# Attention, a dense layer and eight experts on one core: the softmax sums' reciprocals side by side, and the tails' transpose in another PSUM bank

## The chip, the cores and the metric

The kernel runs on one core of one Trainium2 chip. The metric is the device time of one execution in microseconds, as a median of several runs. A profile is one execution taken by the hardware profiler; its span goes from the first to the last instruction.

## The reference

All tensors are float32. The first of three parts is the one that the change touches.

```python
def _attn_ref(q, k, v):                       # 4 batches, 8 heads, 576 positions, 64 features
    scores = scale * np.matmul(q, k.transpose(0, 1, 3, 2))
    mask = block_i >= block_j                 # blocks of 64 positions, block-causal
    scores = np.where(mask, scores, -1000000000.0)
    scores = scores - np.max(scores, axis=-1, keepdims=True)
    attn = np.exp(scores)
    attn = attn / (np.sum(attn, axis=-1, keepdims=True) + 1e-09)
    return np.matmul(attn, v)
...
x = attn_out.transpose(0, 2, 1, 3).reshape(2304, 512)
h = x @ w_in                                  # 512 x 2048
x = np.maximum(0.01 * h, h) @ w_out           # 2048 x 512
P = exp(x @ w_gate - max), 8 rounds of row and column normalisation
out = sum over 8 experts of P[:, e] * (relu(x @ w1[e]) @ w2[e])
```

## The kernel before

Attention works on pairs of heads: 4 batches x 4 pairs = 16 pairs, two heads of 64 features on the 128 partitions. A pair's 576 positions are nine blocks of 64. The loop over pairs p (L471) is software-pipelined over four pairs at once: `prv` = p - 1, `cur` = p, `nxt` = p + 1 and `fol` = p + 2. The list `turns` (L437) is the order in which PE takes one turn of that loop, written out by hand; the order of the other engines and of the DMA queue is made by the framework's planner, from modelled costs.

In one turn, in PE's order: the scores of `nxt` for block 8 and its exponentials; group 0 of the transposed exponentials of `cur`; products of `prv` with v; scores 3 and 2; the rest of the products of `prv`, then `split_x`; group 1; scores 5 and 4; group 2; `turn_q` of `fol`; scores 1 and 0; `turn_tail` of `fol`; the first product of `cur` (L402 and the first of L405); group 3; scores 7 and 6; `turn_k` of `fol`; groups 4, 5 and 6.

`turn_q`, `turn_k` and `turn_tail` transpose q, k and the last 64 positions of both on PE. ACT copies the q side from PSUM into qT (L278), DVE the k side into kT (L283). `turn_attn` transposes 25 pieces of the exponentials in seven groups of four (the last holds one) and copies each group into `at`, even groups on ACT (L390), odd ones on DVE (L392).

A row's sum of exponentials comes out of ACT's exponential, one column of `ssum` for each block. `totals` (at the head of a turn) adds 1e-9 on POOL, takes the reciprocal on DVE (L358) and writes the result to a DRAM tile, the blocks of even and of odd number in a transfer each (L362). `spread_totals` reads each half back with a broadcast over 64 partitions (`by_feature`, four transfers, L371). `split_x` (L414) multiplies the product by it on DVE on its way out of PSUM, and then splits the result into two parts (L424, L425) that the dense layer uses.

PSUM has eight banks: three for scores (`ps_sc`), three for transposes (`ps_tr`, tag `tr`), and one tile of two banks for the product (`ps_av`, tile `av`), in its first bank columns 0 to 127 for the tails, 128 to 255 for the last group of turned rows and 384 to 511 for the first product.

All transfers of this part are issued by SyncE (SP) on one queue, one after the other: q, tails and k three pairs ahead, v, rows, by_feature, and raw weights for the dense layer, whose preparation runs in small steps between the scores. An instruction of SP that waits holds up all that stand behind it.

Behind attention follow the dense layer (L513, L533) and the experts, which the change does not touch.

Of the kernel before, what the change touches and what calls it, by code (L numbers as in the profile page):

```python
# [8 lines left out]
F32 = mybir.dt.float32  # L9
# [6 lines left out]
P = 128  # L16
# [20 lines left out]
def block_attention_mlp_moe(  # L37
# [15 lines left out]
    nc = tc.nc  # L53
# [4 lines left out]
    NQ = S // BLK  # L58
# [156 lines left out]
    def attention(att, ps_sc, ps_tr, ps_av):  # L215
# [13 lines left out]
        ex = [att.tile([P, ew], F32, name=f"ex{i}") for i in range(2)]  # L229
        nmax = [att.tile([P, NQ + 1], F32, name=f"nmax{i}") for i in range(2)]  # L230
        ssum = [att.tile([P, NQ + 1], F32, name=f"ssum{i}") for i in range(2)]
        rsum = [att.tile([P, NQ], F32, name=f"rsum{i}") for i in range(2)]
        NPAR = ((NQ + 1) // 2, NQ // 2)
        by_feature = [[att.tile([P, BLK * n], F32, name=f"by_feature{i}{n}") for n in NPAR] for i in range(2)]
        xs = att.tile([P, S], F32, name="xs")
# [40 lines left out]
        def spread(p, src, lo, n):  # L276
            scale = 1.0 / float(D) ** 0.5
            nc.scalar.activation(  # L278
                out=qT[p % 2][:, lo * BLK:(lo + n) * BLK], in_=src[:, 0:n * BLK], func=AF.Copy, scale=scale
            )  # L280

        def place_k(p, src, lo, hi):
            nc.vector.tensor_copy(out=kT[p % 2][:, lo:hi], in_=src)  # L283
# [3 lines left out]
        def av_tile(p):  # L287
            if p not in av:
                av[p] = ps_av.tile([P, 1024], F32, name="av", tag="av")
            return av[p]  # L290
# [11 lines left out]
            place_k(p, km[:, 0:W], 0, W)  # L302

        def turn_tail(p):
            if 0 <= p - 2:
                tail = av_tile(p - 2)
            else:
                tail = ps_tr.tile([P, 512], F32, name="qk_tail", tag="tr")
            nc.tensor.transpose(tail[:, 0:2 * TAIL], tails, ident)
            spread(p, tail, W // BLK, TAIL // BLK)  # L310
            place_k(p, tail[:, TAIL:2 * TAIL], W, S)
# [41 lines left out]
        rows = {}  # L353

        def totals(p):
            r, s = rsum[p % 2], ssum[p % 2][:, 0:NQ]
            nc.gpsimd.tensor_scalar(out=r, in0=s, scalar1=EPS, scalar2=None, op0=ALU.add)
            nc.vector.reciprocal(out=r, in_=r)  # L358
            rows[p] = []
            for c, n in enumerate(NPAR):  # L360
                t = dram.tile([2, BLK * n], F32, name=f"row{c}", tag=f"row{c}")
                nc.sync.dma_start(out=t.rearrange("h (q i) -> (h q) i", i=n), in_=r[:, c:NQ:2])  # L362
                rows[p].append(t)

        def spread_totals(p):
# [67 lines left out]
        def first_product(p):  # L433
# [5 lines left out]
            ("nxt", scores, 3, 2), *other_parts[2:], ("prv", split_x), ("nxt", load_v), ("cur", turn_attn, 1),  # L439
            ("nxt", scores, 5, 4), ("cur", turn_attn, 2), ("fol", turn_q),  # L440
            ("nxt", scores, 1, 0), ("fol", turn_tail), ("cur", first_product), ("cur", turn_attn, 3),
            ("nxt", scores, 7, 6), ("fol", turn_k), ("cur", turn_attn, 4),
            ("cur", spread_totals), ("cur", turn_attn, 5), ("cur", turn_attn, 6),
        ]
        opening = [
            ("nxt", scores, 1, 0), ("nxt", scores, 3, 2), ("nxt", scores, 5, 4), ("nxt", scores, 8),
            ("fol", turn_q), ("nxt", scores, 7, 6), ("nxt", load_v), ("fol", turn_k), ("fol", turn_tail),
        ]

# [13 lines left out]
        turn_q(0)  # L463
        turn_k(0)
        turn_tail(0)
        warm(ps_sc, "sc", 3)
        load_qk(1)
# [3 lines left out]
        for p in range(-1, NP + 1):  # L471
            who = {"prv": p - 1, "cur": p, "nxt": p + 1, "fol": p + 2}
            if 0 <= p < NP:
                totals(p)
            if p == NP:
                first_product(p - 1)
            for w, f, *a in (turns if p >= 0 else opening):
                if 0 <= who[w] < NP and (f is not first_product or p < NP - 1):
                    f(who[w], *a)
                if f is scores and p >= 0 and steps:  # L480
                    with ExitStack() as queued:
                        if p + 1 < NP:
                            queued.enter_context(tc.issue_after(getattr(latest[0], "ins", latest[0])))
                        steps.pop(0)()
            if p + 3 < NP:
                load_qk(p + 3)
# [50 lines left out]
    with (  # L537
        tc.tile_pool(name="att", bufs=1) as att,
        tc.tile_pool(name="ps_sc", bufs=3, space=bass.MemoryType.PSUM) as ps_sc,
        tc.tile_pool(name="ps_tr", bufs=3, space=bass.MemoryType.PSUM) as ps_tr,  # L540
        tc.tile_pool(name="ps_av", bufs=1, space=bass.MemoryType.PSUM) as ps_av,
    ):
        with tc.manual_schedule(engines={mybir.EngineType.PE}):
            attention(att, ps_sc, ps_tr, ps_av)
# [677 lines left out]
    for n in range(0, NGR, 2):  # L1222
        p, e, i = groups[n]
# [135 lines left out]
```

## Time and profile before

| | us |
|---|---|
| median of 3 runs | 2152.67 |
| lowest and highest run | 2151.68, 2157.7 |
| the profiled execution, its own time | 2158.2 |
| its span | 2156.4 |

The granted TensorE clock is 0.984 of full speed over the span. In the rows below, the waits name the waiting engine and line, then what released it, the total in us, the number of waits and the longest one. A window's columns are its length, then for each engine the busy time and the number of instructions, then the granted clock, the DMA share and GB/s. In a timeline the first two columns are start and length, the last in brackets the idle time before an instruction and what ended it.

### The profile page before, as it was taken

The page shows a single profiled execution, that of the slowest core. Times are in us where ns is not written, and L with a number is a line of the kernel's source. Part 1 is how long each engine was busy: PE and PEld are TensorE (multiplying, and loading weights), DVE is VectorE, ACT ScalarE, POOL GpSimd, SP SyncE. Part 2 cuts the span into 40 slices and gives each one's busy share as a digit, 9 for nine tenths or more (in the row PEclk, how much of TensorE's full clock was granted, in tenths as well). Part 3 has the DMA queues.
Part 4 walks back from the last instruction along what each step waited for, and adds up shares of the span by engine and source line. Part 5 has one row for each costly group of instructions (what it writes and reads, how often), then busy time and mean ns, then how long its engine had stood idle before and what let it go on. Part 6 is the DMA issues. An engine that isn't in the chain of part 4 may idle for free.

```text
span 2156.4 us, 32438 instructions
## 1 busy us (share of the span) xinstructions
PE 2082.3 (97%) x11498; PEld 1862.6 (86%) x11498; DVE 1562.7 (72%) x2687; ACT 815.8 (38%) x1795; POOL 652.2 (30%) x639
## 2 busy tenths in 40 slices
PE   8877789999999999999999999999999999999999
PEld 4434458888888888988998999999999999999998
DVE  5555546575645888778778678888888688888886
ACT  5544423222223544544544433233333433333222
POOL 1211213131301354455445133323332223333322
PEclk9988899999999999999999999999999999999999
DMA  5453421120102788888889877777777677777772
GB/s 114 77 85 71 76 41 51 30 68 23 56 10 103 278 303 300 295 309 304 300 299 339 306 254 265 260 259 247 264 266 284 234 253 255 277 256 263 262 260 109
DMA packets 254945, 436.92 MB, mean 203 GB/s; under 512 B 95016, under 2 KB 135976, under 8 KB 254528
## 3 DMA queue, kind: packets, MB, share of 16 engines
q1 hardware_dynamic: 253584, 434.56, 60.8%
q8 instruction: 91, 1.49, 0.3%
q14 instruction: 70, 0.57, 0.1%
q10 hardware_dynamic: 1200, 0.30, 0.1%
HBM read 308.82 MB, written 125.95 MB: 202 GB/s over the span
## 4 chain that ended last, share of the span: by engine, by line
PE 87%; DMA 6%; DVE 4%; ACT 1%; issue 1%; SPq 1%; POOL 0%; DVEq 0%; ACTq 0%; POOLq 0%
PE h_ps L854 28%; PE o L1022 20%; PE o L1078 13%; PE o L533 9%; PE h_ps L513 9%; PE o L854 3%; DMA row<-rsum 3%; PE sc L331 2%; DMA kraw<-in_k_dram 1%; PE av L405 1%; PE tr L383 1%; DVE nmax L337 1%; DMA by_feature<-row 1%; ACT ex L344 1%; SPq L371 0%
## 5 line engine op out<-in xcount | busy, mean ns | idle before, releaser
L951 DVE TENSOR_TENSOR xa<-o,xa 128x384 f32<-128x384 f32 x392 | 216.0, 552 | 110.5 <-PE o L1022 106.4
L854 PE MATMUL h_ps<-xhS,w1h 128*128 128x384 f32 x768 | 257.5, 335 | 0.0
L854 PE MATMUL h_ps<-xhS,w1l 128*128 128x384 f32 x768 | 256.6, 334 | 0.0
L854 PE MATMUL h_ps<-xlS,w1h 128*128 128x384 f32 x768 | 256.6, 334 | 0.0
L951 POOL TENSOR_TENSOR xa<-xa 128x384 f32<-128x384 f32 x92 | 106.1, 1153 | 408.7 <-DVE xa L951 371.4
L951 ACT COPY places<-h_ps 128x384 f32<-128x384 f32 x192 | 92.3, 481 | 287.1 <-PE h_ps L854 219.5
L951 ACT CAST xllate<-xa 128x384 fp32r<-128x384 f32 x120 | 61.7, 514 | 280.1 <-POOL xa L951 280.1
L854 PE MATMUL h_ps<-xhA,w1h 128*128 128x384 f32 x448 | 150.9, 337 | 2.0 <-DVE c L871 2.0
L854 PE MATMUL h_ps<-xhA,w1l 128*128 128x384 f32 x448 | 149.9, 335 | 0.0
L854 PE MATMUL h_ps<-xlA,w1h 128*128 128x384 f32 x448 | 149.9, 335 | 0.0
L854 PEld LDWEIGHTS h_ps<-xhS,w1h 128*128 128x128 f32 x768 | 144.2, 188 | 0.7 <-issue 0.6
L854 PEld LDWEIGHTS h_ps<-xlS,w1h 128*128 128x128 f32 x768 | 144.2, 188 | 0.0
L854 PEld LDWEIGHTS h_ps<-xhS,w1l 128*128 128x128 f32 x768 | 144.2, 188 | 0.0
L1078 PE MATMUL o<-w2h,xhlate 128*128 128x512 f32 x408 | 143.8, 391 | 0.0
L951 POOL TENSOR_TENSOR places<-places 128x384 f32<-128x384 f32 x60 | 60.9, 1015 | 251.3 <-DVE wa L951 234.6
L1078 PE MATMUL o<-w2h,xllate 128*128 128x512 f32 x384 | 133.9, 389 | 0.0
L1022 PE MATMUL o<-xllate,w2h 128*128 128x384 f32 x480 | 123.2, 336 | 0.3 <-DVE xllate L951 0.2
L1022 PE MATMUL o<-xhlate,w2h 128*128 128x384 f32 x480 | 121.7, 334 | 0.0
L768 POOL TENSOR_TENSOR wa<-wraw 128x256 f32<-128x256 f32 x32 | 29.1, 910 | 300.5 <-DVE w1l L786 277.7
L521 DVE TENSOR_TENSOR g<-h_ps,g 128x512 f32<-128x512 f32 (+1 forms) x80 | 50.9, 637 | 93.2 <-ACT g L520 92.9
L533 PE MATMUL o<-hh,w2h 128*128 128x512 f32 (+1 forms) x320 | 118.0, 369 | 0.0
L533 PE MATMUL o<-hh,w2l 128*128 128x512 f32 (+1 forms) x320 | 117.7, 368 | 0.0
(261 smaller groups left out, 5750.1 us busy)
## 6 DMA issues: line engine op xcount, KB each, us to landing
wraw<-in_moe_w_dram SPq DMA_DIRECT2D x64, 512.0 KB, 4.0
w1h<-k_1h SPq DMA_DIRECT2D x64, 512.0 KB, 5.7
w1l<-k_1l SPq DMA_DIRECT2D x64, 512.0 KB, 6.3
w2h<-k_1h SPq DMA_DIRECT2D x60, 512.0 KB, 6.1
w2l<-k_1l SPq DMA_DIRECT2D x60, 512.0 KB, 6.5
w1h<-k_0h SPq DMA_DIRECT2D x64, 384.0 KB, 3.5
w1l<-k_0l SPq DMA_DIRECT2D x64, 384.0 KB, 4.6
w2h<-k_0h SPq DMA_DIRECT2D x60, 384.0 KB, 4.8
```

The lines of the kernel that those rows point to most:

```text
L331: nc.tensor.matmul(sc[o:o + BLK, :], qT[p % 2][r, i * BLK:(i + 1) * BLK], kT[p % 2][r, lo:hi], start=True, stop=True,)
L337: latest[0] = nc.vector.tensor_reduce(out=nm[:, i + s:i + s + 1], in_=sc, axis=AX.X, op=ALU.max, negate=True)
L344: nc.scalar.activation(out=ex[p % 2][:, off[i] + lo:off[i] + hi], in_=sc, func=AF.Exp, bias=x, scale=1.0, accum_out=sm[:, i + s:i + s + 1],)
L383: nc.tensor.transpose(tr[:, s].rearrange("p h q -> p (h q)"), ex[p % 2][:, off[i] + c * P:off[i] + (c + 1) * P], swap if i in crossed else ...
L513: nc.tensor.matmul(ps[:, 0:n], w[:, c, cols], x, start=c == 0 and s == 0, stop=c == KC - 1 and s == 2,)
L521: nc.vector.tensor_tensor(out=g[:, 0:n], in0=ps[:, 0:n], in1=g[:, 0:n], op=ALU.max)
L533: nc.tensor.matmul(ps[:, 0:n], w[:, cut], h[:, 0:n], start=start and m == 0, stop=stop and m == 2)
L768: nc.gpsimd.tensor_tensor(out=one[:, 0], in0=a21, in1=a22, op=ALU.add)
L854: mm = nc.tensor.matmul(ps, w[:, c], x[:, c], start=first and c == 0 and s == 0, stop=c == 1 and s == 2, skip_group_check=True,)
L951: ins = f(*a, **k)
L1022: mm = nc.tensor.matmul(o, a, b, start=i == 0, stop=i == 5)
L1078: mm = nc.tensor.matmul(o, h, w, start=m == 0, stop=m == 11)
```

## The change

The tile of the reciprocals gets two rows of five columns instead of nine columns: row 0 holds the blocks of even number, row 1 those of odd number. `totals` reads `ssum` with the parity as the outer index, ten columns instead of nine, so that what a partition sends in one transfer lies side by side. `turn_tail` takes a bank of `ps_tr` for every pair; before, it did so for pairs 0 and 1 alone and used the tile `av` of pair p - 2 for the others. The numbers of banks in the three pools stay.

```diff
-        rsum = [att.tile([P, NQ], F32, name=f"rsum{i}") for i in range(2)]
+        rsum = [att.tile([P, 2, (NQ + 1) // 2], F32, name=f"rsum{i}") for i in range(2)]
...
         def turn_tail(p):
-            if 0 <= p - 2:
-                tail = av_tile(p - 2)
-            else:
-                tail = ps_tr.tile([P, 512], F32, name="qk_tail", tag="tr")
+            tail = ps_tr.tile([P, 512], F32, name="qk_tail", tag="tr")
             nc.tensor.transpose(tail[:, 0:2 * TAIL], tails, ident)
...
         def totals(p):
-            r, s = rsum[p % 2], ssum[p % 2][:, 0:NQ]
+            r, s = rsum[p % 2], ssum[p % 2].rearrange("p (i c) -> p c i", c=2)
             nc.gpsimd.tensor_scalar(out=r, in0=s, scalar1=EPS, scalar2=None, op0=ALU.add)
             nc.vector.reciprocal(out=r, in_=r)
...
-                nc.sync.dma_start(out=t.rearrange("h (q i) -> (h q) i", i=n), in_=r[:, c:NQ:2])
+                nc.sync.dma_start(out=t.rearrange("h (q i) -> (h q) i", i=n), in_=r[:, c, 0:n])
```

## Rows read from the trace of the kernel before

**Rows 1.** The page: the chain that ended last, by engine

```profile
PE 87%; DMA 6%; DVE 4%; ACT 1%; issue 1%; SPq 1%; POOL 0%; DVEq 0%; ACTq 0%; POOLq 0%
```

**Rows 2.** Windows: the turns of attention, its end, and the rest

```profile
core 0: us, PE busy (x) PEld busy (x) DVE busy (x) ACT busy (x) POOL busy (x), PEclk, DMA share, GB/s
22.08:256.40 234.32, 184.53 (x1280) 96.43 (x1274) 131.68 (x292) 110.51 (x363) 43.00 (x57) 0.88 0.48 80
256.40:298.48 42.08, 28.99 (x193) 16.14 (x189) 16.03 (x34) 14.57 (x46) 6.18 (x8) 0.84 0.39 46
298.48:2156.40 1857.92, 1849.80 (x9911) 1738.28 (x9910) 1402.58 (x2325) 678.91 (x1350) 598.94 (x552) 1.00 0.63 222
```

**Rows 3.** Waits of PE from 22.08 to 256.40 us, all there are

```profile
PE av L402 <- DVE kT L283: 17.6, 13, 1.9
PE qm L295 <- DMA qraw<-in_q_dram: 13.3, 6, 3.5
PE sc L331 <- ACT ex L344: 7.1, 14, 1.2
PE sc L331 <- DVE kT L283: 6.5, 11, 1.0
PE km L301 <- DMA kraw<-in_k_dram: 5.3, 3, 2.5
```

**Rows 4.** Waits of PE from 256.4 to 298.48 us, the longest

```profile
PE sc L331 <- ACT ex L344: 5.1, 2, 3.9
PE tr L383 <- DVE at L392: 4.6, 1, 4.6
PE av L402 <- DVE kT L283: 1.8, 1, 1.8
```

**Rows 5.** Timeline of SP, one round from by_feature to by_feature

```profile
60.90 2.41 SPq L371 DMA_DIRECT2D by_feature<-row  x4
...
67.25 1.26 SPq L362 DMA_DIRECT2D row<-rsum  x2
...
71.12 0.54 SPq L136 DMA_DIRECT2D wraw<-in_moe_w_in_dram  x1
78.14 2.37 SPq L371 DMA_DIRECT2D by_feature<-row  x4
```

**Rows 6.** Waits of SP from 22.08 to 256.40 us, the longest

```profile
SPq L371 <- DMA row<-rsum: 81.3, 18, 7.7
```

**Rows 7.** DMA issues of the span: count, KB each, median us to landing

```profile
k_1l<-wraw SPq DMA_DIRECT2D x32, 256.0 KB, 2.5
...
tails<-in_q_dram SPq DMA_DIRECT2D x16, 32.0 KB, 2.4
...
row<-rsum SPq DMA_DIRECT2D x16, 2.5 KB, 10.2
row<-rsum SPq DMA_DIRECT2D x16, 2.0 KB, 12.9
```

**Rows 8.** Windows: two turns, from one turn of the tails to the next

```profile
54.49:69.63 15.14, 12.38 (x102) 6.79 (x98) 10.68 (x25) 8.68 (x29) 4.40 (x6) 1.00 0.41 75
...
181.10:199.90 18.80, 15.34 (x101) 7.52 (x99) 10.47 (x23) 8.63 (x30) 3.30 (x6) 0.83 0.42 83
```

**Rows 9.** Timeline around the tails' transpose of one undisturbed turn

```profile
54.07 0.58 ACT L390 COPY at<-tr 128x512 f32<-128x512 f32 x1
...
54.49 0.33 PE L309 MATMUL av<-ident,tails 128*128 128x128 f32 x1
...
55.81 0.22 DVE L283 COPY kT<-av 128x64 f32<-128x64 f32 x1 [0.27 <-ACT qT L278]
...
56.09 0.44 PE L402 MATMUL av<-at,vraw 128*64 128x128 f32 x4 [1.27 <-DVE kT L283]
...
57.21 0.33 PE L383 MATMUL tr<-swap,ex 128*128 128x128 f32 x1
```

**Rows 10.** The tile rsum: duration ns min/median/max, first and last start

```profile
L357 POOL TENSOR_SCALAR rsum<-ssum x16: 242/242/294, 15.9 to 283.8; 128x9 f32<-128x9 f32 x16
L358 DVE RECIPROCAL rsum<-rsum x16: 202/206/217, 16.2 to 284.1; 128x9 f32<-128x9 f32 x16
```

## The prediction

> **What bounds the kernel now.** I read four views in turn: where the time of the chain lies, how busy each engine is before and after the attention part, what TensorE (PE) waits for there, and what SyncE's queue (SP) does meanwhile. Over the whole span the chain is mostly PE, with a few per cent of DMA [rows 1]. The windows split that: from 298.48 us on PE is busy 1849.80 of 1857.92 us, so nothing is to be had there, and nothing of that part is edited. From the first turn of the tails at 22.08 to the last at 256.40 PE is busy only 184.53 of 234.32 us, and from there to the first matmul of the dense layer 28.99 of 42.08 [rows 2]. The change can act on these 276 us alone. The first stretch holds 13 turns of the loop over pairs: 234.32 / 13 = 18.02 us each.
>
> The idle time of PE in those 13 turns is 49.8 us, and five waits make it up: 17.6 us in which the first product (L402) waits for the copy of the tails (kT, L283), 13.3 and 5.3 us for late loads of q and k, 7.1 and 6.5 us for ACT's exponentials and DVE's copies [rows 3]. In the last 42 us there are 4.6 us behind DVE's copy L392, 5.1 us behind ACT (3.9 of it in one wait) and 1.8 us behind the tails' copy [rows 4].
>
> Why the loads of q and k are late is in SP's own order. SP issues everything in one line: by_feature (L371), q, tails and k of a later pair, the row transfers (L362), v, sometimes raw weights, and then it stands before the next by_feature until the rows have landed. In the turn shown it issues by_feature at 60.90, the rows at 67.25, is done with the last issue at 71.66 and goes on at 78.14: 17.24 us for the round, of which 6.48 are that wait [rows 5]. Over the 13 turns it stood there for 81.3 us [rows 6]. The landing is the reason: the 640 runs of 4 bytes of the first row transfer need 10.2 us, the 512 of the second 12.9, where 32 KB of tails land in 2.4 [rows 7]. So SP's round of 17 to 18 us sets the turn in most of the loop; where nothing is late, the turn takes 15.14 us [rows 8].
>
> **The change part by part.** *Rows sent whole.* The reciprocals of one parity now lie side by side, so a partition's 5 (or 4) values go as one run of 20 (or 16) bytes: 128 and 128 runs for 640 and 512. No row here shows such a transfer. From below: 2.4 us, the tails' load of 128 runs. From above: no gain, 12.9. Between them I price by runs: a store of 256 KB into DRAM lands in 2.5 us [rows 7], which I take as the fixed part; 10.2 - 2.5 over 640 runs is 12 ns a run, and for both transfers together (12.9 + 0.6 for the later issue - 2.5) over 1152 is 10 ns. Both new ones, 256 runs, then land 2.5 + 3 = 5.5 us (estimate) after the first issue. In the turn shown that is 72.8 in place of 78.1: SP's round falls from 17.24 to about 12, under the 14 to 15 us that PE needs. Then q and k are no longer late: 13.3 + 5.3 = 18.6 us. At the end, L392 stood behind split_x, which waited for by_feature, which waited for the rows; these 4.6 us go, and the 3.9 us behind ACT have the same root: 8.5 us. What is late next is not SP: after the rows it has some 2 us to spare per turn.
>
> The Trainium skill ("DMA: Bandwidth & Descriptors", Anatomy of one DMA) says that a DMA has a fixed cost of about 2 us, most of it the receipt from the memory written, and that with HBM this can be surprisingly long. The 2.5 us of the 256 KB store [rows 7] agree with its figure; if the long receipt were the cause of the 10 us, the landing would stay, which is the third case below.
>
> *Tails in a bank of their own.* Now the transpose of the tails (L309) writes the bank of av that the first product uses next. In the undisturbed turn it starts at 54.49 and runs 0.33; DVE's copy, behind ACT's, starts at 55.81, and L402 goes at 56.09 after 1.27 us of waiting. What L402 truly needs, the copy of turned rows by ACT at 54.07 for 0.58, ended at 54.65 [rows 9]. With the tails in a tr bank L402 can go right behind the transpose, at about 54.85. Nothing of the 1.27 us is left over, so I take all 17.6 + 1.8 = 19.4 us. What queues behind it, turned rows and the next scores, moves forward with it. The tr banks are now used nine times a turn and not eight: the fourth group of turned rows takes the bank of the third, free at 54.65 and wanted at about 55.97 (it starts at 57.21 now, 1.12 us after L402); the fifth group takes the tails' bank, free at 56.03 and wanted only behind the next scores and the turn of k. The first has 1.3 us of cover, the second more, and if that went, the excess would be paid on PE, turn by turn.
>
> *Ten columns for nine.* POOL's addition (242 ns) and DVE's reciprocal (206 ns) read one column more [rows 10]: 16 of each, an eleventh longer at most, 16 x 0.04 = 0.7 us. It is hidden: the rows have several microseconds before split_x wants them.
>
> *The clock.* PE's granted clock in the 13 turns is 0.88 on average: stretches at 2.4 GHz with stretches at 1.2 between them [rows 2]. A turn at 1.00 holds 12.38 us of PE work, one at 0.83 holds 15.34 [rows 8]; 13 x 12.38 = 161 against 184.5 leaves 23.6 us that the slow stretches cost. They follow waits of PE, and about three quarters of the waits go; but the undisturbed turns have dips too, and 13.6 us of waits on ACT and DVE stay. Between 0 and 23.6 I take a third, 7.9.
>
> **Sum.** 18.6 + 8.5 + 19.4 + 7.9 = 54.4 us; the turn comes to (234.3 - 36.2 - 7.9) / 13 = 14.6 us, near the 15.14 - 1.27 = 13.9 of the undisturbed turn less its wait. The profiled execution took 2158.2 us (span 2156.4 and 1.8 around it), 5.5 above the median of the runs, so this reads 2103.8 for such an execution and 2152.7 - 54.4 = 2098 for the median.
>
> **The rivals.** *Second: half the landing.* The runs get fewer but each dearer, and the rows land after some 8.5 us. SP's round is then about 16.2 us and still sets the turn; what the tails give is waited for elsewhere. 13 x (18.0 - 16.2) + 6 at the end = 29: 2123, in a band of 2115 to 2140. For it: the second transfer, with fewer runs than the first, lands later still, so the runs of a transfer by themselves don't set its time. Against: the tails' load, with as many runs as each new one, lands in 2.4 [rows 7].
>
> *Third: the landing does not change,* because its price goes by the words written or by the receipt. Then SP still takes 18 us, and the tails' 1.27 us become a longer wait for q. Only the early turns, where SP was not yet behind, keep their gain: three or four of 1.27, some 5 us, 2147. The 2.5 us of the large store speak against it, and nothing in the trace shows a 20-byte run.
>
> *Fourth, on the other side: the tr banks.* If ACT's copy of the third group comes over 1.3 us later than in the undisturbed turn, the fourth group waits on PE where it did not before. To end slower by 0.3% (6.5 us) it must be late by 1.3 + 1.27 + 0.5 = 3.1 us in each of 14 turns, with nothing won from the rows. ACT is busy 110.51 of 234.32 us [rows 2], so it is late only where it waits for DVE behind split_x, and that grows rarer. Time 2160.
>
> **Chances.** The first case 0.76 (0.04 of it below 2082), the second 0.13, the third 0.08, the fourth 0.03. If the whole 23.6 us of the clock come back, the time is 2152.7 - 46.5 - 23.6 = 2082.6; that is the low end. The high end, 2126, takes in about half of the second case. A change of less than 0.3% (6.5 us) is about what this measurement can't tell from none. Faster: 0.76 + 0.13 + 0.02 of the third = 0.91; same 0.06; slower 0.03.
>
> **What will show it.** The landing of the row transfers near 5 us, and SP's wait before by_feature a small part of 81 us; the waits of PE for q and k gone; L402 no longer behind L283; tails' turns 14 to 15 us apart; a mean granted clock above 0.88; the first matmul of the dense layer near 244 us and the part after it as long as before (1858 us). The forecast is wrong if the rows still land after 8 us or more, if the fourth or fifth group of turned rows waits for a bank, or if the planned order of SP's queue changes so that a load is put behind a wait for the rows.

## The result, and the profile after

| | us |
|---|---|
| before, median of 4 runs | 2152.18 (2150.47 to 2157.7) |
| after, median of 4 runs | 2086.69 (2086.47 to 2087.5) |
| ratio | 0.9692, 95% interval 0.9674 to 0.971 |
| after, the profiled execution and its span | 2086.56, 2084.8 |

The changed kernel is faster by 65.5 us; the prediction said 54.4 (2098, range 2082 to 2126). On the chips of the experiments the kernel before has medians of 2136.4 to 2139.0 and the changed one 2085.5 to 2086.9, so there the same change gives 52 to 53.5 us. Each ratio below is to runs of the kernel before on the same chip; where rows of two chips stand side by side, the text says so. One execution of the kernel with one parity at a distance took 6279.8 us at a granted clock of 1.00 and is left out of its median below.

Past the edit all line numbers are 3 lower: L306 is the transpose of the tails, L328 the scores, L359 the row transfers, L368 by_feature, L399 the first product, L402 the rest of the products. The rows of each experiment have the lines of its own kernel; with the rows alone they are those of the kernel before.

The windows, cut at the same instructions as [rows 2]: first and last turn of the tails, first matmul of the dense layer.

```profile
core 0: us, PE busy (x) PEld busy (x) DVE busy (x) ACT busy (x) POOL busy (x), PEclk, DMA share, GB/s
21.96:198.94 176.98, 160.98 (x1281) 88.35 (x1275) 131.32 (x292) 109.97 (x363) 43.01 (x57) 1.00 0.46 109
198.94:227.05 28.11, 24.05 (x192) 13.89 (x189) 15.94 (x34) 14.51 (x46) 6.13 (x8) 1.00 0.25 62
227.05:2084.80 1857.75, 1850.00 (x9910) 1738.82 (x9910) 1402.26 (x2325) 678.85 (x1350) 598.30 (x552) 1.00 0.63 222
```

The rest is as long as it was (1857.75 against 1857.92). The 13 turns went from 234.32 to 176.98, 13.61 us each, and the end from 42.08 to 28.11. In both, PE does the same matmuls in less busy time, and the granted clock is 1.00: the engine is at 2.4 GHz throughout. PE's waits, first in the 13 turns (all there are, against [rows 3]), then one of the five of the end (against [rows 4]):

```profile
PE sc L328 <- DVE kT L283: 9.4, 13, 1.0
PE sc L328 <- ACT ex L341: 6.6, 15, 0.6
```

```profile
PE tr L380 <- DVE at L389: 0.6, 1, 0.6
```

The waits for q and k are gone, and so is that of the first product for the tails' copy. None of the groups of turned rows makes PE wait for a bank inside the turns. SP's waits from 0 to 227.05 us, two of the rows:

```profile
SPq L246 <- PE av L402: 37.0, 14, 4.0
...
SPq L368 <- DMA row<-rsum: 2.0, 4, 0.7
```

SP stood 81.3 us for the rows in 13 turns [rows 6], now 2.0. What holds it now is the other direction: its loads of v (L246) wait until PE has read the buffer. The DMA issues (count, KB each, median us to landing) and one round of SP:

```profile
vraw<-in_v_dram SPq DMA_DIRECT2D x32, 128.0 KB, 2.6
...
row<-rsum SPq DMA_DIRECT2D x16, 2.5 KB, 2.5
row<-rsum SPq DMA_DIRECT2D x16, 2.0 KB, 2.7
```

```profile
48.44 2.46 SPq L368 DMA_DIRECT2D by_feature<-row  x4
...
55.95 0.81 SPq L359 DMA_DIRECT2D row<-rsum  x2
59.93 0.38 SPq L246 DMA_DIRECT2D vraw<-in_v_dram  x1
...
62.84 2.38 SPq L368 DMA_DIRECT2D by_feature<-row  x4
```

The rows land about as fast as the tails do (10.2, 12.9 and 2.4 us in [rows 7]). So do the loads of v, which stand right behind the rows in SP's queue. In the same view of before they land late, though PE had no wait for v there [rows 3]:

```profile
vraw<-in_v_dram SPq DMA_DIRECT2D x32, 128.0 KB, 11.3
```

SP's round is 14.40 us here, but it holds 3.17 us (56.76 to 59.93) in which SP waits for PE: PE sets the turn. Around the tails' transpose, against [rows 9]:

```profile
49.70 0.33 PE L306 MATMUL qk_tail<-ident,tails 128*128 128x128 f32 x1
...
49.96 0.44 PE L399 MATMUL av<-at,vraw 128*64 128x128 f32 x4
...
51.01 0.22 DVE L283 COPY kT<-qk_tail 128x64 f32<-128x64 f32 x1 [0.27 <-ACT qT L278]
...
51.08 0.33 PE L380 MATMUL tr<-swap,ex 128*128 128x128 f32 x1
```

The first product goes 0.26 us after the transpose, 1.05 us before DVE's copy of the tails, and the fourth group of turned rows follows at 51.08, again 1.12 us behind it, without a wait.

### The profile page after: what moved, and what is told of

Its sections match the earlier page's. It is cut to its first block, busy times and chain, and to the rows that moved or that the text cites. A ratio compares the mean times of both kernels' runs of the same rounds, so it can differ in the third digit from the quotient of the medians.

```text
span 2084.8 us, 32437 instructions
## 1 busy us (share of the span) xinstructions
PE 2053.9 (99%) x11498; PEld 1852.8 (89%) x11498; DVE 1561.9 (75%) x2687; ACT 815.1 (39%) x1795; POOL 651.5 (31%) x639
## 4 chain that ended last, share of the span: by engine, by line
PE 91%; DVE 5%; issue 2%; ACT 1%; POOL 1%; DMA 1%; SPq 0%; DVEq 0%; ACTq 0%; POOLq 0%
PE h_ps L851 29%; PE o L1019 21%; PE o L1075 12%; PE o L530 10%; PE h_ps L510 10%; PE o L851 3%; PE sc L328 2%; PE av L402 1%; DVE nmax L334 1%; PE tr L380 1%; ACT ex L341 1%; DVE xs L411 0%; DVE at L389 0%; DVE kT L283 0%; DMA k_1h<-wb 0%
```

## The experiments

### One part at a time

The rows alone keep the tails where they were:

```diff
-            tail = ps_tr.tile([P, 512], F32, name="qk_tail", tag="tr")
+            if 0 <= p - 2:
+                tail = av_tile(p - 2)
+            else:
+                tail = ps_tr.tile([P, 512], F32, name="qk_tail", tag="tr")
```

> The rows go as runs of 20 and 16 bytes, the tails stay in the product's bank. Theory (SP's round set the turn, the tails' wait is a separate 1.27 us a turn, and the waits for late loads are what mostly pulls the granted clock down): rows land in 2.5 to 3 us, SP's wait before by_feature is a few us in all, no wait of PE for q or k, the first product still waits about 1.27 us behind the tails' copy; the turn is near 15 us, the granted clock between 0.93 and 1.00, the time about 2110 (2102 to 2120), some two thirds of the whole gain of 65. Rival (the bank is what frees the turn, the rows are hidden): 2135 or more.

Measured: 2120.34 us against 2136.37, ratio 0.9923 (0.9903 to 0.9943), at the slow edge of what was expected. The rows land in 1.6 and 2.5 us and PE never waits for q or k. PE's waits in its 13 turns, and the windows of all 13 and of two of them:

```profile
PE av L402 <- DVE kT L283: 18.5, 13, 2.1
PE sc L331 <- DVE kT L283: 8.8, 13, 1.0
PE sc L331 <- ACT ex L344: 6.6, 15, 0.6
```

```profile
21.85:231.21 209.36, 175.51 (x1281) 93.16 (x1275) 131.38 (x292) 109.96 (x363) 42.92 (x57) 0.93 0.38 92
...
53.97:70.45 16.48, 13.97 (x99) 7.42 (x99) 10.95 (x25) 8.67 (x29) 4.39 (x6) 0.90 0.31 73
70.45:84.97 14.52, 12.38 (x99) 6.79 (x99) 9.14 (x21) 8.15 (x28) 1.83 (x4) 1.00 0.49 119
```

The mean turn is 16.1 us, not near 15. Behind the first, a turn has two lengths: 14.5 to 15.2 us where PE's matmuls take 12.4, and 15.8 to 17.1 where they take 14.0 at a mean clock of 0.9. Nine of the 13 turns are of the second kind. In the turn from 53.97 the first product waits 1.26 us, until 55.82; the windows behind it:

```profile
54.23:57.00 2.77, 1.51 (x14) 0.61 (x10) 1.27 (x5) 1.93 (x9) 0.10 (x1) 1.00 0.35 114
57.00:60.40 3.40, 3.40 (x17) 1.47 (x16) 1.10 (x2) 0.00 (x0) 0.00 (x0) 0.50 0.43 95
60.40:70.71 10.31, 9.06 (x76) 5.33 (x75) 8.31 (x19) 6.74 (x20) 4.30 (x5) 1.00 0.26 56
```

PE is busy all through the 3.40 us at 0.50 (1.2 GHz): the fall of the clock comes after the wait, while there is work, and costs about half of 3.4, the 1.6 us by which PE's busy time differs between the two kinds of turn. From this kernel to the changed one (profiles of two chips) the 13 turns lose 209.36 - 176.98 = 32.4 us: 17.9 of waits (33.9 to 16.0) and 14.5 of PE busy time (175.51 to 160.98). So it isn't mostly the late loads that pull the clock down, as I had expected: without them PE's busy time falls by 9.0 us (184.53 in [rows 2] to 175.51, two chips again), and the larger part comes back only with the bank.

The bank alone keeps nine columns and the runs of 4 bytes:

```diff
-        rsum = [att.tile([P, 2, (NQ + 1) // 2], F32, name=f"rsum{i}") for i in range(2)]
+        rsum = [att.tile([P, NQ], F32, name=f"rsum{i}") for i in range(2)]
...
-            r, s = rsum[p % 2], ssum[p % 2].rearrange("p (i c) -> p c i", c=2)
+            r, s = rsum[p % 2], ssum[p % 2][:, 0:NQ]
...
-                nc.sync.dma_start(out=t.rearrange("h (q i) -> (h q) i", i=n), in_=r[:, c, 0:n])
+                nc.sync.dma_start(out=t.rearrange("h (q i) -> (h q) i", i=n), in_=r[:, c:NQ:2])
```

> The tails go to a tr bank, the rows stay runs of 4 bytes. Theory: SP's round of 17 to 18 us still sets the turn; the 1.27 us come back as longer waits for q and k; rows land in 10 us or more, clock 0.85 to 0.92 in the turns; time 2140 to 2152. Rival (the two gains add up): 2152 - 65 + what the rows alone give, near 2130 or less.

Measured: 2138.75 us, ratio 1.0008 (0.999 to 1.0025): no difference, a little below the time expected. PE's longest wait of its turns, and SP's:

```profile
PE qm L295 <- DMA qraw<-in_q_dram: 27.1, 9, 4.4
```

```profile
SPq L368 <- DMA row<-rsum: 62.3, 15, 7.2
```

The wait for the tails' copy is gone here too, and PE stands for q instead: SP's round still sets the turn (17.2 us). So where the rows give 16 us and the bank nothing, both together give 50 (2136.4 to the 2086.7 and 2086.9 that the changed kernel takes, on two other chips). The parts are not to be added: the tails' wait costs time only once SP no longer does, and the clock comes back in full only when both waits are gone (or, further down, the second is filled with work).

### What the landing depends on

One parity at a distance: the blocks of odd number lie 8 bytes apart again, so 512 runs of 4 bytes and 128 of 20 are sent for 256 runs.

```diff
-        rsum = [att.tile([P, 2, (NQ + 1) // 2], F32, name=f"rsum{i}") for i in range(2)]
+        rsum = [att.tile([P, 2, NQ + 1], F32, name=f"rsum{i}") for i in range(2)]
...
+            near, apart = r[:, 0, 0:half], r[:, 1, 0:2 * half:2]
...
+                nc.sync.dma_start(out=t.rearrange("h (q i) -> (h q) i", i=n), in_=(near, apart)[c][:, 0:n])
```

> The changed kernel, but the odd blocks' reciprocals lie 8 bytes apart again, so that 512 of the runs are of 4 bytes and 128 of 20 (POOL's addition and DVE's reciprocal are two instructions each). Theory (the landing is priced by runs, and only what goes beyond SP's spare time lengthens the turn): the odd row lands in 6 to 8 us, SP stands some 3 us a turn before by_feature, and the turn is 13.6 to 14.6 us: 2088 to 2103. Rival (any clogging by 4-byte runs slows the loads of the whole queue in proportion): about half of the gain is lost, 2115 or more.

Measured: 2137.51 us, ratio 1.0003 (0.9988 to 1.0018): the whole gain is lost, more than the half that the slower of the two cases expected. Its loads of v and its rows, and SP's wait in its 13 turns:

```profile
vraw<-in_v_dram SPq DMA_DIRECT2D x32, 128.0 KB, 7.7
...
row<-rsum SPq DMA_DIRECT2D x16, 2.0 KB, 8.5
row<-rsum SPq DMA_DIRECT2D x16, 2.5 KB, 9.2
```

```profile
SPq L371 <- DMA row<-rsum: 68.5, 12, 8.7
```

One transfer of 4-byte words is enough to hold the round at 16.1 us. The words (2.0 KB) go first in SP's queue here, and what follows is late as well: the 20-byte runs right behind them land in 9.2 us, where they took 2.5 in the changed kernel, and the loads of v in 7.7 (2.6 there). PE doesn't wait for v here either; whether this holding up of other transfers costs time beside SP's standing, no run separates. The landing alone doesn't refute the prediction's price, for 2.5 us and 10 ns for each of 640 runs would be 8.9. The price was therefore measured by itself, with everything else left out: small transfers from SBUF to DRAM, one at a time, each read back (L49) before the next. In the first of the four rounds the planner let other transfers run beside them; the ranges below leave that round out. It also sent the eight loads meant to stand behind a transfer within the first 16 us, over 200 us ahead of it, so rival B's loads were not tested. The core of the first probe, which writes zeros as its output:

```python
t = dram.tile([P, 5], F32)           # 128 runs of 20 bytes, L60
nc.sync.dma_start(out=t, in_=r[:, 0:5])
...
t = dram.tile([P, 1], F32)           # 128 words side by side, L63
nc.sync.dma_start(out=t, in_=r[:, 0:1])
...
t = dram.tile([P, 5, 16], F32)       # 640 words, 64 bytes apart, L69
nc.sync.dma_start(out=t[:, :, 0], in_=r[:, 0:5])
```

> Transfers from SBUF to DRAM measured by themselves, each waited for before the next; the rest of the computation is left out and the output is zeros. Forms: 640, 512, 256 and 128 words of 4 bytes from places 8 bytes apart to a dense block, 128 runs of 20 bytes to a dense block, 640 words from dense places to words 64 bytes and 512 bytes apart in DRAM, 512 runs of 512 bytes; then 640 words, and 128 runs of 20 bytes, with a load of 128 KB right behind them. Theory (the landing is priced by the number of writes that share a short stretch of DRAM): 640 dense words 8 to 10 us, 128 runs 2 to 3 us, 640 words 512 bytes apart clearly less than 640 dense ones. Rival A (by runs, wherever they go): the three forms of 640 within 20% of each other. Rival B (alone, short runs cost little; only the loads behind them in the queue make them slow): 640 dense words under 4 us alone.

> This kernel leaves the whole computation out (it writes zeros) and only sends small transfers from SBUF to DRAM one at a time, each read back before the next is sent: 640 words of 4 bytes at a distance of 8, 16, 32 and 64 bytes from each other, 128 runs of 8, 16, 32 and 64 bytes side by side, 2048 words side by side of which 16 in a row come from one partition, and 640 words side by side of which 5 in a row come from one partition. Theory: a write to DRAM that shares a 64-byte stretch with other writes waits for them, and the landing grows with the number of writes that share a stretch. From the first probe (32 words that shared stretches of 16, 7 us; words 64 bytes apart, 2.5 to 3.2 us) that gives 4 to 5 us at 8 bytes, 3 to 4 at 16, about 3 at 32 and 2.5 at 64; the runs of 8 bytes 4 us, of 16 bytes 2 to 3, of 32 and 64 bytes 1.5 to 2; both of the last two 7 to 10. Rival one: the stretch is shorter, 32 bytes or less; then 32 bytes apart costs as little as 64, and the runs of 16 bytes as little as the runs of 64. Rival two: the price is that of a 4-byte write whatever its neighbours, and what the first probe showed at 64 bytes has another reason; then all four distances cost the same.

From the first probe's timeline of SP; the time from a write's issue to the issue that reads it back is the landing:

```profile
84.64 0.35 SPq L60 DMA_DIRECT2D runs<-r  x1
87.60 0.21 SPq L49 DMA_DIRECT2D back<-runs  x1
89.00 0.34 SPq L63 DMA_DIRECT2D words<-r  x1
96.41 0.21 SPq L49 DMA_DIRECT2D back<-words  x1
...
108.07 0.52 SPq L69 DMA_DIRECT2D spread<-r  x1
111.07 0.62 SPq L49 DMA_DIRECT2D back<-spread  x1
```

128 runs of 20 bytes take 2.96 us here (1.4 to 3.0 in all), 128 words side by side 7.41 (6.9 to 7.5), and 640 words 64 bytes apart 3.00 (2.5 to 3.2). 512 words side by side take 6.5 to 6.8, 640 of them 8.1 to 9.6. So neither the number of runs nor the bytes set the price, but how the writes lie to each other in DRAM. (The dense 512 and 640 words are also read 8 bytes apart from SBUF, the spread ones side by side; the 128 words, one from each partition, are not, and take 7 us.) The second probe varies the distance; its waits of SP over all four rounds (us in total, times, longest):

```profile
SPq L49 <- DMA dense5by<-r: 33.0, 4, 9.8
SPq L49 <- DMA pitch8by<-r: 15.1, 4, 4.5
SPq L49 <- DMA pitch16by<-r: 12.2, 4, 3.8
SPq L49 <- DMA runs8by<-r: 10.3, 4, 2.7
SPq L49 <- DMA pitch32by<-r: 9.4, 4, 2.9
SPq L49 <- DMA pitch64by<-r: 8.6, 4, 2.3
...
SPq L49 <- DMA runs16by<-r: 4.7, 4, 1.5
...
SPq L49 <- DMA runs32by<-r: 4.3, 4, 1.1
SPq L49 <- DMA runs64by<-r: 4.2, 4, 1.1
```

For 640 words the wait falls from 8.25 us side by side (33.0 / 4) to 3.8, 3.0, 2.4 and 2.2 at 8, 16, 32 and 64 bytes. For 128 runs side by side it is 2.6 us at 8 bytes and 1.1 to 1.2 from 16 bytes on. The four distances came about where the theory put them. The runs didn't quite: those of 8 bytes land in 2.9 to 3.1 us where 4 was expected, and those of 16 bytes cost nothing extra, though four of them share 64 bytes, which is what rival one said; but by that rival words 32 bytes apart would cost no more than words 64 apart, and their landings differ (2.9 to 3.5 us against 2.6 to 2.9). How long the stretch is stays open. The 2048 words, sixteen in a row from one partition, land in 11.5 to 13.6 us, above the 10 expected. What is shown is that words of 4 bytes side by side are by far the dearest, whether each comes from another partition (the 128 of the first probe) or sixteen in a row from one, and that runs of 16 bytes or more (up to the 64 measured) are free of it.

### SP's standing still, without a word of 4 bytes

Two more copies of the rows inside DRAM before by_feature reads them; rows and copies land in 1.8 to 2.8 us, but SP has four more transfers to issue in a turn and must wait for the rows and again for the first copy.

```diff
+            for hop in range(2):
+                for c, n in enumerate(NPAR):
+                    t = dram.tile([2, BLK * n], F32, name=f"hop{hop}{c}", tag=f"hop{hop}{c}")
+                    nc.sync.dma_start(out=t.rearrange("h (q i) -> (h q) i", i=n),
+                                      in_=rows[p][c].rearrange("h (q i) -> (h q) i", i=n))
+                    rows[p][c] = t
```

> The changed kernel, but by_feature is read from a copy of a copy of the rows: two more pairs of transfers from DRAM to DRAM stand one behind the other in SP's queue, with no run of 4 bytes anywhere. Theory (it is enough that SP stands still: its round goes to 16 or 17 us, so q and k come late and PE's granted clock falls): turn 15.5 to 17.5 us, waits of PE for q or k of 10 us or more, 2110 to 2140. Rival (4-byte runs do harm by clogging the transfer engines for the loads, SP's standing alone is hidden): turn within 0.5 us of the changed kernel's 13.6, at most 2095.

> The changed kernel itself, as a measure for its variants on the same chip. The time of before differs by 16 us between two chips (2152 and 2136), that of a kernel that waits for no transfer should not: 2085 to 2089, with the turn at 13.6 us.

Measured: 2109.05 us, against 2086.9 for the changed kernel run beside it; the turn takes 15.24 us. SP's waits of its 13 turns (L364 issues the copies), and PE's for q and for the tails of k; then the window of the 13 turns:

```profile
SPq L364 <- DMA row<-rsum: 23.3, 15, 3.7
SPq L364 <- DMA hop<-row: 9.9, 12, 2.1
```

```profile
PE qm L295 <- DMA qraw<-in_q_dram: 5.1, 7, 1.7
PE qk_tail L306 <- DMA tails<-in_k_dram: 3.9, 4, 1.9
```

```profile
21.32:219.41 198.09, 170.28 (x1279) 90.96 (x1275) 132.44 (x293) 111.20 (x366) 43.05 (x57) 0.96 0.39 94
```

Time, turn and waits (9.0 us for 10 or more) are a little under what was expected, but the loads are late again, the mean clock of the turns falls to 0.96, and 22 us are lost to SP's longer round alone, well above the 2095 of the rival.

### The wait filled with work

The rows alone once more, with nine matmuls on constants (results unused) between the tails' transpose and the first product.

```diff
-            ("nxt", scores, 1, 0), ("fol", turn_tail), ("cur", first_product), ("cur", turn_attn, 3),
+            ("nxt", scores, 1, 0), ("fol", turn_tail), ("fol", fill), ("cur", first_product), ("cur", turn_attn, 3),
```

> The rows sent whole and the tails left in the product's bank, with nine small matmuls on zeros (about 1.1 us, into a tr bank that nobody reads) where PE waits for the tails' copy. Theory (with the rows whole, what pulls the granted clock down is PE's idle time around that wait): the wait behind the copy shrinks to about 0.2 us while the time in the turn stays as long, the dips to 0.5 go, PE's other work in the 13 turns needs 161 us as in the changed kernel: turn about 15.0, 2104 to 2110 against 2120 without the filler. Rival (the dips have another cause): the filler is added work and the clock stays: 2118 to 2125.

Measured: 2112.1 us, ratio 0.988 (0.986 to 0.99), 2 us above the upper end of what was expected. Its 13 turns:

```profile
21.48:224.57 203.09, 186.84 (x1514) 114.33 (x1508) 131.53 (x292) 109.96 (x363) 42.95 (x57) 1.00 0.39 95
```

The clock is 1.00 in all 13 turns, where it was 0.93 without the filler (on another chip), and PE with nine more matmuls a turn (two records each) is through 6.3 us sooner (203.09 against 209.36). A turn is 15.62 us, more than the 14.5 of an undisturbed one, since the filler is longer than the wait that it fills: (186.84 - 160.98) / 13 = 2.0 us a turn for 18.5 / 13 = 1.4. That the falls of the clock follow PE's idle wait is shown by this and by their absence where the wait is taken away; why four turns of the rows alone had the wait and no fall stays open.

### What is left, and a faster version

The waits that remain name their cure: the scores 7 and 6 wait for DVE's copy of k, so the transpose of k can go ahead of them; then those for ACT's exponential are left, and the tails' transpose can go into that gap.

```diff
-            ("nxt", scores, 7, 6), ("fol", turn_k), ("cur", turn_attn, 4),
+            ("fol", turn_k), ("nxt", scores, 7, 6), ("cur", turn_attn, 4),
```

> The changed kernel with the turn of k one place earlier in the written order, ahead of scores 7 and 6. Theory (in the changed kernel PE's longest wait is for DVE's copy of kT, 10.3 us in all, and that copy stands behind two reductions of the scores): the wait mostly goes, 0.5 to 0.7 us a turn, 2078 to 2083. Rival (the reductions of scores 7 and 6 are pushed back by as much, and the exponentials after them hold up the groups of the next turn): 2086 to 2092.

```diff
-            ("nxt", scores, 1, 0), ("fol", turn_tail), ("cur", first_product), ("cur", turn_attn, 3),
+            ("fol", turn_tail), ("nxt", scores, 1, 0), ("cur", first_product), ("cur", turn_attn, 3),
```

> The kernel with the turn of k ahead of scores 7 and 6, and now the turn of the tails ahead of scores 1 and 0 as well. In the turns of that kernel the only wait of PE that is left is that of the scores for ACT's exponential, 8.7 us in 17 waits, and the larger part of it is before scores 1 and 0. Theory: the tails' transpose needs a bank of turned rows that is free by then, so 0.1 us of work at each of 13 turns goes into the wait, and the wait shrinks by that: 1 to 4 us of 2078, so 2074 to 2077. Rival: the transpose only moves, what comes behind it is then the first product, which waits for the tails' copy on DVE, or the wait is not before these scores: 2078 or more.

> The kernel with the turn of k ahead of scores 7 and 6, once more, beside the next one on the same chip: 2078 in both theories.

> The changed kernel itself, on the same chip: 2087 in both theories, and so 8 to 9 us above the kernel with the turn of k moved.

| on one chip | median, us | ratio to before |
|---|---|---|
| changed kernel | 2085.49 (2084.21 to 2086.29) | 0.9747 (0.9733 to 0.9762) |
| turn of k ahead | 2079.08 (2078.94 to 2079.72) | 0.9719 (0.9703 to 0.9735) |
| turn of the tails ahead as well | 2075.49 (2074.76 to 2076.42) | 0.9701 (0.9687 to 0.9716) |

An earlier run of the second, on another chip, gave 2078.15. The second's only wait of PE in the 13 turns, and the longer of the third's two (the other is 0.2 us in all):

```profile
PE sc L328 <- ACT ex L341: 8.7, 17, 1.4
```

```profile
PE sc L328 <- ACT ex L341: 7.0, 16, 1.4
```

The wait for DVE's copy of k is gone, and that for ACT's exponential is longer (6.6 in the changed kernel). The first move gives 6.4 us beside the changed kernel, where 8 to 9 were expected, the second 3.6, within the 1 to 4 expected. The second takes 3.6 us off the 13 turns (171.42 to 167.83), of which 1.5 stand in the waits and 2.1 in PE's busy time, whose ends are modelled.

## Why the prediction was right, and what was mis-sized

The mechanism was the one predicted: SP's round lost its wait, the first product lost its own, and PE sets the turn. By terms, on the profiled executions:

| term | predicted | measured | from |
|---|---|---|---|
| waits of the 13 turns | 36.2 | 33.8 | 49.8 to 16.0 |
| waits of the end, tails among them | 10.3 | 9.0 | 42.08 - 28.99 to 28.11 - 24.05 |
| clock in the 13 turns | 7.9 | 23.5 | PE busy 184.53 to 160.98 |
| clock at the end | 0 | 4.9 | PE busy 28.99 to 24.05 |
| sum | 54.4 | 71.2 | the span lost 71.6 |

The profiled execution of before took 6.0 us more than its median, so 71.6 reads as 65.6 between medians, the 65.5 measured. The prediction took terms read from that slower execution straight off the median: against the profiles its sum is 16.8 us short, against the medians 11.1, and that difference is luck. It is luck too that 54.4 lies near the 52 to 53.5 us of the later chips, since before is faster there to begin with.

- **Late loads (18.6):** right; both waits are gone.
- **Tails (19.4):** the wait is gone as a whole, but the scores behind it now wait 9.4 us in the turns for DVE's copy of k where they waited 6.5, and 0.9 at the end. These 2.9 us more, less 0.5 of ACT's, are the 2.4 by which the turns' waits missed; I had looked for what is late next in the banks and on SP, and it was in this copy.
- **The end (8.5):** right within 1.3 us; the 4.6 us behind L392 are 0.6.
- **Ten columns (0):** right for PE, which doesn't wait for the sums. SP does now, 10.1 us in all for DVE's reciprocals before it sends the rows, but it has that room.
- **The clock (7.9):** this is the mis-sized term. I took a third of 23.6 because undisturbed turns had dips too and 13.6 us of waits stay. All 23.5 came back, and 4.9 at the end that I hadn't counted, though [rows 2] show 0.84 there. The undisturbed turns of before still held the first product's wait of 1.27 us; rows alone shows that this wait goes with a fall in nine turns of 13, and the filler that without it there is none. The 16.0 us that stay come in waits of 1.0 us at most, and in this kernel no fall follows them. The 2082.6 that I gave for the whole clock, as the low end of the range, is 4 us from the result.
- **The landing (5.5 us, estimated by runs):** the wrong price with the right sign. It goes by how the writes lie to each other, and the 256 runs of 16 and 20 bytes land in 2.5 and 2.7 us, about as the tails' load does. The 2.5 us taken as the fixed part were also the fastest of the stores of 256 KB: in the same view of before the others land in 3.8 to 6.6. Because SP had room from about 12 us a round on, the three us in between changed nothing in the sum.
- **The rivals:** half the landing needed 8.5 us, and one parity at a distance shows what that gives: nothing at all, not the 29 us I worked out. There the rows land after 8.5 and 9.2 us, PE waits 17.6 us for q, and the clock in the turns is 0.92. The working had a slip besides: by the times of [rows 5] a landing of 8.5 us makes a round of 14.9 us, not 16.2. A landing that doesn't change would have been the bank alone, 2138.75 against 2136.37: no gain, where I had 5 us. The banks of turned rows cause no wait in the turns. The Trainium skill ("DMA: Bandwidth & Descriptors", Anatomy of one DMA), on transfers issued by GpSimd, puts most of a fixed 2 us on the receipt from the memory written; the landings of 1.4 to 3.0 us of the 20-byte runs, issued by SP, agree with that size. The 128 words and the 128 runs are as many writes into the same memory, and the words take 7 us, so a fixed receipt isn't what made the rows late. The Trainium skill (the same page, Specifications) says that below 512 bytes a write becomes a read and a write; 4 and 20 bytes are both below, so that rule doesn't tell apart what the probe does.

What stays open is why the kernel before takes 2152 us on one chip and 2136 to 2139 on others while the changed one agrees within 1.5 us on three. The granted clock of before, 0.984 in the first profile against 0.986 to 0.989 in the runs on the later chips, points to the falls of the clock; no run here tests it.

## What to carry to other kernels

Look at how the writes of a small transfer lie in DRAM before looking at its bytes: a stride of 8 bytes in SBUF that splits a row into 4-byte words cost 8 to 10 us a transfer here, and one queue issued in order passes that on to the loads behind it. When two waits share a turn, price them together: taken singly they gave 16 and 0 us, together 50, and short waits of PE cost their length and then again in the granted clock (from the rows alone to the whole change 17.9 and 14.5 us). After such a change read PE's remaining waits by the instruction that ends them; two moves in the written-out order then gave another 10 us.

## What the runs showed of the hardware

- 128 words of 4 bytes side by side in DRAM land in 6.9 to 7.5 us, 128 runs of 20 bytes in 1.4 to 3.0, and 640 words 64 bytes apart in 2.5 to 3.2. 128 runs of 8 bytes side by side take 2.9 to 3.1 us, of 16, 32 and 64 bytes 1.4 to 2.0.
- Behind a transfer of 512 words of 4 bytes in SP's queue, 128 runs of 20 bytes landed in 9.2 us and loads of 128 KB in 7.7, where without such words they took 2.5 and 2.6.
- A wait of PE of 1.26 us was followed by 3.40 us at a granted clock of 0.50 while PE was busy without a gap (57.00 to 60.40 with the rows alone). Nine of 13 turns with a wait at that line had such a fall; with the rows sent whole and that wait filled or taken away, the clock in the turns stays at 1.00.
